# Backward pass of a transformer block: the gradient of w_qkv with its operands exchanged, and y's residual added by GpSimd

## The chip, the cores and the metric

The kernel runs on one core of one Trainium2 chip. The metric is the device time of one execution in microseconds (us); runs of one kernel are compared by the median. The engines are PE (TensorE, with PEld for its weight loads), DVE (VectorE), ACT (ScalarE), POOL (GpSimd) and SP (SyncE, which here only issues DMAs).

## What is computed

A block of attention and a gated feed-forward layer stand side by side on the normalised input, and the kernel returns the block's output and the gradients of six inputs for a given grad_out. S = 2048 rows, D = 448 columns, 16 heads of 28, F = 1792, all in bfloat16.

```python
def block(x, wqkv, wo, w_gate, w_up, w_down):
    xn = layernorm(x)
    q, k, v = split_heads(xn @ wqkv)          # 16 heads of 28
    p = softmax(q @ k.T * 28 ** -0.5)
    attention = merge_heads(p @ v) @ wo
    ffn = (silu(xn @ w_gate) * (xn @ w_up)) @ w_down
    return x + attention + ffn

out, vjp = jax.vjp(block, x, wqkv, wo, w_gate, w_up, w_down)
return (out, *vjp(grad_out))
```

The change touches two results: `out_2`, the gradient of wqkv (448 x 1344, xn transposed times the gradients of q, k and v), and `out_0`, the block's output y.

## The kernel before

A tile framework allocates the buffers and sets the semaphores; the order of the instructions on each engine is the one in which the code calls them. Heads are handled in four groups of four; each head is padded from 28 to 32 rows, so that a group fills 128 partitions. The rows of x are cut into 16 tiles of 128 (`NT`).

**Forward and feed-forward part** (up to about 673 us). Projections, the forward softmax and the feed-forward layer with its weight gradients. Its intermediate results go to DRAM: `hd_d` holds, per row tile, the transposed attention output and the transposed hidden activations; `qT_d`, `kT_d`, `vT_d`, `dOT_d` and `spq_d`, `spk_d`, `spo_d` hold what the backward attention reads.

**Backward loop** (lines 627 to 918). A unit is one pair of heads, one quarter (512) of the keys and one tile of 128 query rows; there are 512 units (`units`), and eight of them make a window `W`, with position `pos` 0 to 7 in it. Per unit PE computes scores and dP (`sd`, L851 and L862), ACT the exponential `E` (L869), DVE `ds` = dP times E (L880), and PE accumulates the gradients of k and v (`acc_mm`, L748, four matmuls on 32 columns of the array each). Six of eight `ds` tiles are transposed by DMA from SP (L882, `dsT<-ds`), the other two by PE (L775, copied out in L782); from `dsT` PE makes the gradient of q once per window (`dq_mm`, L795), and DVE adds it up (`dq_out`). There are eight `ds` buffers. When a pair is done, its gradients lie in `dsp[pr]`: `dkv_sp` with v and k by row tile (transposed by SP, L761) and `dq_sp` with q (L817).

**Jobs.** Other work for PE is spread over positions 1 to 4 of each window, one job a window by the list `jobs` (`None` is a window without one): `y` computes a row tile of the output, 18 matmuls of 448 columns and a nineteenth that adds x through the identity matrix; `dx` a row tile of two partial input gradients, 14 matmuls; `dwq` the gradient of wqkv for one group `g` and one chunk `c` of 128 of the 448 rows. Before, `dwq` has the chunk of xn as the weights and moves the gradients, 128 columns (k and v of one pair) or 64 (q of one pair) at a time. Its result (384 columns) is copied by ACT (`dwq_raw`), put in order by six POOL copies (`dwq_z`) and written by one DMA. A job's chunk of `hd_d` is loaded by SP two windows ahead (`job_load`, `ck` and `x_c`).

**SP's queue** carries, in this order of calls, the chunk loads at position 0, the loads of the next pair, group and weights (`load_pair`, `load_group`, `load_w`) at position 4, the `ds` transposes, and what is in the list `sp_later` (the transposes L761 and L817), which is emptied once a unit. In the built program each transfer of this queue also waits for the landing of an earlier one with which it shares a semaphore.

**The end** (lines 921 to 980). The fourth group's `dwq` is computed without a window, partly in the loop's last steps and partly after it (`last_dwq`), in two of the three PSUM buffers `sd`. Then come 16 rows of the input gradient: 2 + 12 matmuls of 448 columns on `pab` (partial sums) and `dq_c` (gradients of q, k, v from DRAM), a normalisation backward on ACT and DVE, and the addition of grad_out by POOL (`dx`, L979), written by SP. Their loads are issued by SP (`load_c` for chunks 0 to 2) and ACT.

Of the kernel before, what the change touches and what calls it, by code (L numbers as in the profile page):

```python
# [10 lines left out]
ALU = mybir.AluOpType  # L11
AX = mybir.AxisListType
FP32 = mybir.dt.float32
BF16 = mybir.dt.bfloat16
# [16 lines left out]
DCH = [(0, 128), (128, 128), (256, 128), (384, 64)]  # L31
# [6 lines left out]
def kernel(  # L38
# [19 lines left out]
    pe, act, dve, pool, sp = nc.tensor, nc.scalar, nc.vector, nc.gpsimd, nc.sync  # L58
# [22 lines left out]
    ident_bf = const.tile([P, P], BF16, name="ident_bf")  # L81
# [6 lines left out]
    xn_sp = const.tile([P, NT, DP], BF16, name="xn_sp")  # L88
# [39 lines left out]
    for b in (2, 3):  # L128
# [10 lines left out]
        out=r_ones[:], in_=ident_f[:].rearrange("p (a b) -> p a b", b=HP)[:, :, 28:30],  # L139
# [448 lines left out]
    for i, (g, qc, kt) in enumerate(steps):  # L588
# [24 lines left out]
        if i in (6, 8, 10, 12):  # L613
            j = i // 2 - 3
# [12 lines left out]
    cst = ExitStack()  # L627
    dspp = cst.enter_context(tc.tile_pool(name="dspp", bufs=3))
    outp = cst.enter_context(tc.tile_pool(name="outp", bufs=2))
    ps_sd = cst.enter_context(tc.tile_pool(name="ps_sd", bufs=3, space=PSUM))  # L630
    ps_x = cst.enter_context(tc.tile_pool(name="ps_x", bufs=1, space=PSUM))
    ast = ExitStack()
# [11 lines left out]
    N = len(units)  # L644
    NW = N // UW
    chunk, dsp, dqacc = {}, {}, {}


    jobs = [None] + [("y", t) for t in range(NT)] + [None] + [("dwq", 0, c) for c in range(4)]
    jobs += [("dx", 0, t) for t in range(NT)] + [("dwq", 1, c) for c in range(4)]  # L650
    jobs += [("dx", 1, t) for t in range(8)] + [None] + [("dwq", 2, c) for c in range(4)]
    jobs += [("dx", 1, t) for t in range(8, NT)]

    def job_load(i):
        if i >= len(jobs) or jobs[i] is None:
# [12 lines left out]

    def dwq_mms(g, c, ps):

        out = []
        lhs = lambda t: xn_sp[:, t, c * P:(c + 1) * P]

        def kvm(t):
            for hp in range(2):
                pe.matmul(ps[:, hp * P:(hp + 1) * P], lhsT=lhs(t), rhs=dsp[2 * g + hp][0][:, t, :],
                          start=(t == 0 and hp == 0), stop=(t == NT - 1), skip_group_check=True)

        def qm(t):
            for hp in range(2):  # L680
                pe.matmul(ps[:, 256 + hp * 64:256 + hp * 64 + 64], lhsT=lhs(t),
                          rhs=dsp[2 * g + hp][1][:, t // 8, t % 4, t % 8 // 4, :],
                          start=False, stop=(t == NT - 1), skip_group_check=True)
        for f in (kvm, qm):
            out.append([lambda t=t, f=f: f(t) for t in range(NT)])
        return out

    def dwq_out(g, c, ps):
        d0, dn = DCH[c]
        o = outp.tile([P, 384], BF16, name="dwq_raw")  # L690
        act.copy(out=o[:], in_=ps[:, :384])
        z = outp.tile([P, 3, 4, DH], BF16, name="dwq_z")
        kv = o[:, :256].rearrange("p (h v j r) -> p h v j r", h=2, v=2, r=HP)
        for tq in range(3):
            for hp in range(2):
                src = (o[:, 256 + 64 * hp:320 + 64 * hp].rearrange("p (j r) -> p j r", r=HP) if tq == 0
                       else kv[:, hp, 2 - tq])
                pool.tensor_copy(out=z[:, tq, 2 * hp:2 * hp + 2, :], in_=src[:, :, :DH])
        pool.dma_start(
            out=out_2[d0:d0 + dn, :].rearrange("p (t c) -> p t c", t=3)[:, :, g * 4 * DH:(g + 1) * 4 * DH],  # L700
            in_=z[:dn].rearrange("p t h d -> p t (h d)"))

    def job_mms(i, ps):
        j = jobs[i]
        if j[0] == "dwq":
            return sum(dwq_mms(j[1], j[2], ps), [])
        if j[0] == "y":
            t, x = chunk[i]
            out = []
            for n in range(NFC + G):  # L710
                rhs = (wo_pad[:, n, :D] if n < G else wtile["wd"][:, n - G, :])
                out.append(lambda n=n, rhs=rhs: pe.matmul(ps[:, :D], lhsT=t[:, n, :], rhs=rhs,  # L712
                                                          start=(n == 0), stop=False))
            out.append(lambda: pe.matmul(ps[:, :D], lhsT=ident_bf[:], rhs=x[:], start=False, stop=True))
            return out
        t = chunk[i]
        w = wtile[("wg", "wu")[j[1]]]
        return [lambda n=n: pe.matmul(ps[:, :D], lhsT=t[:, n, :], rhs=w[:, n, :],  # L718
                                      start=(n == 0), stop=(n == NFC - 1)) for n in range(NFC)]

    def job_out(i, ps):
        j = jobs[i]
        if j[0] == "dwq":
            dwq_out(j[1], j[2], ps)
            return
        o = outp.tile([P, D], BF16, name="row_o")
        act.copy(out=o[:], in_=ps[:, :D])
        if j[0] == "y":
            pool.dma_start(out=out0_d[:, j[1], :], in_=o[:])
        else:  # L730
            pool.dma_start(out=(pA_d, pB_d)[j[1]][:, j[2], :], in_=o[:])
        if j[0] != "dwq" and j[-1] == NT - 1 and j[:2] != ("dx", 1):
            wload.extend(load_w("wg" if j[0] == "y" else "wu", 7))

    E, DS, st = {}, {}, {}
    sp_later = []

    def acc_mm(k):
        pr, kc, w, qi = units[k]
# [89 lines left out]
    fillers, last_dwq = [], []  # L829
    for k in range(N + 2 * UW):  # L830
        W, pos = k // UW, k % UW
        if k < N:
            pr, kc, w, qi = units[k]
# [13 lines left out]
            q, kv = qd[pr]  # L847
            qt = 8 * w + qi
            s_ps = ps_sd.tile([P, 2, 512], FP32, name="sd")
            for j in range(2):  # L850
                pe.matmul(s_ps[:, j, :], lhsT=q[HP * j:HP * j + HP, qt * P:(qt + 1) * P],  # L851
                          rhs=kv[HP * j:HP * j + HP, kc * 512:(kc + 1) * 512],
                          start=True, stop=True, tile_position=(HP * j, 0))
        late_tr = pos == 0 and 1 <= W <= NW
        if 1 <= k <= N:
            pr, kc, w, qi = units[k - 1]
            q, kv = qd[pr]
            qt = 8 * w + qi
# [34 lines left out]
        if 1 <= pos < 5 and job:  # L893
            n = -(-len(fillers) // (5 - pos))
# [1 line left out]
                f()  # L896
            fillers = fillers[n:]
        if k == N + UW + 5:
            for c in range(4):
                if c % 2 == 0:  # L900
                    g_t = ps_sd.tile([P, 2, 512], FP32, name="sd")
                last_dwq.append((g_t[:, c % 2, :], dwq_mms(3, c, g_t[:, c % 2, :])))
            for _, m in last_dwq:
                for f in m[0][:12]:
                    f()
        if pos == 5 and 2 <= W <= NW + 1:
            dq_mm(W - 2, 0)
# [13 lines left out]
    with ExitStack() as fin:  # L921
# [17 lines left out]
            q.dma_start(out=dq_c[ck][:], in_=dqkv_d[ck])  # L939
        for ck in range(3):  # L940
            load_c(ck, sp)
        for part in range(2):
            for c, (ps, m) in enumerate(last_dwq):
                for f in m[part][12 * (1 - part):]:
                    f()
                if part == 1:
                    dwq_out(3, c, ps)
        wq = wtile["wq"]
        for t in range(NT):
            if t % 2 == 0:  # L950
# [61 lines left out]
```

## Time and profile before

| | |
|---|---|
| median of 3 runs | 1563.34 us (1561.85 to 1567.34) |
| profiled execution, its own time | 1562.89 us |
| span from its first to its last instruction | 1561.1 us |
| granted TensorE clock | 0.976 |
| PE, DVE, ACT, POOL busy | 93%, 70%, 76%, 25% of the span |
| DMA | 285.12 MB, mean 183 GB/s |
| SP's and ACT's transfers (q1) | 210.03 MB, 72.7% of 16 engines |
| first and last exponential of the backward loop | 673 and 1481 us |

A line of a group reads: source line, engine, operation, tile written <- tiles read with their sizes, number of instructions | busy us, mean ns of one | idle us of the engine just before them, and who ended most of it. "SPq" is SP's queue: an entry is the issue of a DMA, not its transfer; "to landing" is the time from issue until the data is there. A busy PE is not PE at its peak, since the ends of pipelined matmuls are modelled.

### The profile page before, as it was taken

To read this page: it belongs to the slowest core of one execution; us is meant where nothing else is said; L and a number is where in the kernel's file an instruction comes from. 1 tells how busy PE (TensorE), PEld (TensorE's weight loads), DVE (VectorE), ACT (ScalarE), POOL (GpSimd) and SP (SyncE) were. 2 spreads that over 40 slices of the span, in tenths; PEclk is the share of its full clock that TensorE was granted. 3 is DMA by queue.
4 is the path that set the end of the run, shared out by engine and by line. 5 is a ranking of instruction groups with operands and counts; after the bars stand their busy time and mean duration, and the time that the engine had idled before them with its cause. 6 is when DMAs were issued, how large, how long until landed. Compare 5 with 4: busy or idle time off the path is not lost.

```text
span 1561.1 us, 32024 instructions
## 1 busy us (share of the span) xinstructions
PE 1447.1 (93%) x12176; PEld 606.3 (39%) x12176; DVE 1098.9 (70%) x1421; ACT 1190.1 (76%) x1333; POOL 396.1 (25%) x664
## 2 busy tenths in 40 slices
PE   6999999899999999988998988989999899999986
PEld 3233333333333333333333444434335333544353
DVE  7664655455655666467877887979888789888925
ACT  6899998688787877766776777878778778888823
POOL 4342333344434444411010111110102111111033
PEclk9999999899999999989999999999999999999998
DMA  9985756875967699879999999999999999999993
GB/s 231 190 162 120 145 116 137 164 146 127 198 131 155 134 186 212 170 164 222 204 214 200 192 202 217 198 197 200 207 208 199 196 194 196 185 188 213 184 281 123
DMA packets 682106, 285.12 MB, mean 183 GB/s; under 512 B 637136, under 2 KB 650464, under 8 KB 681952
## 3 DMA queue, kind: packets, MB, share of 16 engines
q1 hardware_dynamic: 652016, 210.03, 72.7%
q0 software_dynamic: 25968, 64.53, 17.1%
q10 hardware_dynamic: 3968, 8.52, 1.6%
q8 instruction: 95, 1.56, 0.4%
q14 instruction: 59, 0.48, 0.1%
HBM read 67.34 MB, written 63.44 MB: 84 GB/s over the span
## 4 chain that ended last, share of the span: by engine, by line
PE 63%; DMA 14%; ACT 9%; DVE 6%; issue 5%; SPq 1%; POOL 1%; DVEq 0%; POOLq 0%; ACTq 0%
PE s_ps L600 8%; PE f_ps L357 8%; DMA dsT<-ds 8%; PE f_ps L383 7%; PE sd L851 6%; ACT E L869 5%; PE acc L748 4%; PE aux L718 4%; PE o_ps L582 4%; PE aux L775 4%; PE aux L795 4%; DVE ds L880 3%; PE aux L712 3%; ACT dsT L782 3%; PE sd L862 3%
## 5 line engine op out<-in xcount | busy, mean ns | idle before, releaser
L880 DVE TENSOR_TENSOR ds<-sd,E 128x1024 bf16<-128x1024 f32 x512 | 611.2, 1220 | 131.8 <-DMA dsT<-ds 47.8
L869 ACT ACTIVATE E<-sd 128x1024 bf16<-128x1024 f32 x512 | 516.7, 1024 | 171.7 <-PE sd L862 133.6
L604 ACT ACTIVATE eT<-s_ps 128x1024 bf16<-128x1024 f32 x512 | 497.9, 1024 | 103.8 <-PE s_ps L600 102.9
L862 PE MATMUL sd<-kT,qT 32*128 32x512 bf16 x1024 | 203.2, 390 | 23.6 <-ACT E L869 22.7
L851 PE MATMUL sd<-kT,qT 32*128 32x512 bf16 x1024 | 201.9, 391 | 20.1 <-DVE ds L880 17.9
L748 PE MATMUL acc<-ds,v_sp 128*32 128x512 bf16 x1024 | 205.7, 397 | 0.7 <-DVE ds L880 0.7
L748 PE MATMUL acc<-E,O_sp 128*32 128x512 bf16 x1024 | 205.5, 397 | 0.2 <-ACT dkv_o L754 0.2
L600 PE MATMUL s_ps<-qT,kT 32*128 32x512 bf16 x1024 | 200.1, 388 | 1.5 <-ACT eT L604 1.1
L422 POOL DMA_DIRECT2D hd_d<-fT x168 | 126.8, 767 | 17.2 <-DVE fT L407 9.9
L383 PE MATMUL f_ps<-xnT,wgu 128*128 128x512 bf16 x448 | 120.2, 387 | 3.4 <-DVE w_sb L409 3.4
L763 POOL DMA_DIRECT2D dqkv_d<-dkv_o x64 | 39.3, 619 | 293.1 <-ACT dkv_o L754 290.9
L600 PEld LDWEIGHTS <-kT 32*128 32x128 bf16 x1024 | 48.7, 91 | 159.8 <-issue 158.1
L718 PE MATMUL aux<-W,ck 128*128 128x448 bf16 x448 | 107.1, 356 | 3.3
L851 PEld LDWEIGHTS <-qT 32*128 32x128 bf16 x1024 | 51.0, 91 | 149.2 <-issue 141.2
L582 PE MATMUL o_ps<-eT,v_sp 128*32 128x512 bf16 x1024 | 103.2, 394 | 0.0
L357 PE MATMUL f_ps<-xn_sp,f_sp 128*128 128x448 bf16 x448 | 99.1, 354 | 0.0
L748 PEld LDWEIGHTS <-O_sp 128*32 128x32 bf16 x1024 | 50.4, 93 | 113.5 <-issue 103.7
L775 PE MATMUL aux<-ident_bf,ds 128*128 128x128 bf16 x1024 | 81.6, 224 | 11.6 <-DVE dq_acc L807 5.7
L862 PEld LDWEIGHTS <-qT 32*128 32x128 bf16 x1024 | 65.0, 91 | 61.7 <-issue 57.8
L357 PEld LDWEIGHTS <-f_sp 128*128 128x128 bf16 x672 | 58.3, 98 | 73.8 <-issue 23.7
L775 PEld LDWEIGHTS <-ds 128*128 128x128 bf16 x1024 | 63.7, 100 | 40.9 <-issue 40.2
L395 DVE SCALAR_TENSOR_TENSOR g<-t_sb,f_ps 128x512 f32<-128x512 f32 x56 | 38.5, 687 | 55.4 <-ACT t_sb L393 55.3
(133 smaller groups left out, 1759.8 us busy)
## 6 DMA issues: line engine op xcount, KB each, us to landing
hd_d<-fT POOLq DMA_DIRECT2D x168, 128.0 KB, 4.6
ck<-hd_d SPq DMA_DIRECT2D x32, 448.0 KB, 4.4
ck<-hd_d SPq DMA_DIRECT2D x16, 576.0 KB, 4.9
dsT<-ds SPq DMA_TRANSPOSE x384, 4.1
dqkv_d<-dkv_o POOLq DMA_DIRECT2D x64, 64.0 KB, 3.7
dq_c<-dqkv_d ACTq DMA_DIRECT2D x5, 768.0 KB, 6.8
W<-wT_d SPq DMA_DIRECT2D x14, 224.0 KB, 3.6
out_dram<-dw_o POOLq DMA_DIRECT2D x28, 96.0 KB, 4.0
```

The source lines that it names most:

```text
L357: pe.matmul(acc[:, :D], lhsT=src[:, 12 * (t // 4) + 4 * wi + t % 4, :], rhs=rhs[:, t, :D], start=(t == 0), stop=(t == NT - 1))
L383: pe.matmul(st[name][:], lhsT=w(c), rhs=src[:, tsl, c, :], start=(c == 0), stop=(c == 3))
L582: pe.matmul(o_ps[HP * hh:HP * (hh + 1), :], lhsT=v[:, kt, HP * hh:HP * (hh + 1)], rhs=e[hh // 2][:, hh % 2, :], start=(kt == 0), stop=(kt ...
L600: pe.matmul(s_ps[:, j, :], lhsT=kT[r:r + HP, kt * P:(kt + 1) * P], rhs=qT[r:r + HP, qc * 512:(qc + 1) * 512], start=True, stop=True, tile_ ...
L604: act.activation(out=e[:], in_=s_ps[:], func=ACT.Exp, scale=SCALE)
L718: return [lambda n=n: pe.matmul(ps[:, :D], lhsT=t[:, n, :], rhs=w[:, n, :], start=(n == 0), stop=(n == NFC - 1)) for n in range(NFC)]
L748: pe.matmul(acc[r:r + HP, :], lhsT=src[:, qt, 64 * hp + HP * j:64 * hp + HP * j + HP], rhs=m[:, j, :], start=(qt == 0), stop=(qt == NT - 1 ...
L775: pe.transpose(ps[:, i, :], ds[:, i // 4, (i % 4) * P:(i % 4 + 1) * P], ident_bf[:])
L851: pe.matmul(s_ps[:, j, :], lhsT=q[HP * j:HP * j + HP, qt * P:(qt + 1) * P], rhs=kv[HP * j:HP * j + HP, kc * 512:(kc + 1) * 512], start=Tru ...
L862: pe.matmul(d_ps[:, j, :], lhsT=q[r:r + HP, qt * P:(qt + 1) * P], rhs=kv[r:r + HP, kc * 512:(kc + 1) * 512], start=True, stop=True, tile_p ...
L869: act.activation(out=E[k][:], in_=s_ps[:], func=ACT.Exp, scale=SCALE)
L880: dve.tensor_tensor(out=DS[k - 1][:], in0=d_ps[:], in1=E[k - 1][:], op=ALU.mult)
```

## The change

The gradient of wqkv is computed transposed. For group `g` there are now three jobs instead of four: `c` = 0 and 1 are k and v of one pair (16 matmuls, the pair's 128 gradient columns are the weights and xn's 448 columns move), `c` = 2 is q of the whole group (64 matmuls, each with 32 columns of weights on a quarter of the array's columns). ACT copies the 448 columns of the result into one of two fixed buffers, `dwq_w[c % 2]`; SP transposes that by DMA into `dwq_o`; POOL copies the parts into `dwq_z`, and after `c` = 2 issues four DMAs that write the group. The transpose and what follows it are put off through `sp_later`, which is now declared ahead of the loop. The job list follows: windows without a job are 0, 17, 40 and 60 to 63 instead of 0, 17, 50 and 63, and the `dx` jobs start one window earlier. At the end the fourth group's three jobs are worked off one after the other, each with its transposes issued at once.

In `y`, the nineteenth matmul is gone. ACT copies the sum in FP32 (`y_sb`), POOL adds x and writes `row_o`, and the DMA follows as before.

```diff
+    gwp = cst.enter_context(tc.tile_pool(name="gwp", bufs=1))
...
-    jobs = [None] + [("y", t) for t in range(NT)] + [None] + [("dwq", 0, c) for c in range(4)]
-    jobs += [("dx", 0, t) for t in range(NT)] + [("dwq", 1, c) for c in range(4)]
-    jobs += [("dx", 1, t) for t in range(8)] + [None] + [("dwq", 2, c) for c in range(4)]
-    jobs += [("dx", 1, t) for t in range(8, NT)]
+    sp_later = []
+    dwq_w = [gwp.tile([P, DP], BF16, name=f"dwq_w{i}") for i in range(2)]
+    for w in dwq_w:
+        pool.memset(w[:, D:], 0.0)
+    jobs = [None] + [("y", t) for t in range(NT)] + [None] + [("dwq", 0, c) for c in range(3)]
+    jobs += [("dx", 0, t) for t in range(NT)] + [("dwq", 1, c) for c in range(3)] + [None]
+    jobs += [("dx", 1, t) for t in range(9)] + [("dwq", 2, c) for c in range(3)]
+    jobs += [("dx", 1, t) for t in range(9, NT)]
...
         def kvm(t):
-            for hp in range(2):
-                pe.matmul(ps[:, hp * P:(hp + 1) * P], lhsT=lhs(t), rhs=dsp[2 * g + hp][0][:, t, :],
-                          start=(t == 0 and hp == 0), stop=(t == NT - 1), skip_group_check=True)
+            pe.matmul(ps[:, :D], lhsT=dsp[2 * g + c][0][:, t, :], rhs=xn_sp[:, t, :D],
+                      start=(t == 0), stop=(t == NT - 1))
 
         def qm(t):
-            for hp in range(2):
-                pe.matmul(ps[:, 256 + hp * 64:256 + hp * 64 + 64], lhsT=lhs(t),
-                          rhs=dsp[2 * g + hp][1][:, t // 8, t % 4, t % 8 // 4, :],
-                          start=False, stop=(t == NT - 1), skip_group_check=True)
+            for h in range(4):
+                pe.matmul(ps[HP * h:HP * (h + 1), :D],
+                          lhsT=dsp[2 * g + h // 2][1][:, t // 8, t % 4, t % 8 // 4, HP * (h % 2):HP * (h % 2 + 1)],
+                          rhs=xn_sp[:, t, :D], start=(t == 0), stop=(t == NT - 1),
+                          tile_position=(0, HP * h), skip_group_check=True)
+        return [lambda t=t: (kvm if c < 2 else qm)(t) for t in range(NT)]
...
     def dwq_out(g, c, ps):
...
+        w = dwq_w[c % 2]
+        act.copy(out=w[:, :D], in_=ps[:, :D])
+        if c == 0:
+            dwq_z[g] = gwp.tile([P, 4, 3, 4, DH], BF16, name="dwq_z")
+        z = dwq_z[g]
+        o = outp.tile([P, 4, P], BF16, name="dwq_o")
+        def later():
+            sp.dma_start_transpose(out=o[:], in_=w[:])
+            parts = [(0, 0, 4, 0)] if c == 2 else [(2, 2 * c, 2, 0), (1, 2 * c, 2, 64)]
+            for tq, h0, n, c0 in parts:
+                pool.tensor_copy(out=z[:, :, tq, h0:h0 + n, :],
+                                 in_=o[:, :, c0:c0 + HP * n].rearrange("p c (h r) -> p c h r", r=HP)[:, :, :, :DH])
+            if c < 2:
+                return
+            for i, (d0, dn) in enumerate(DCH):
+                pool.dma_start(
+                    out=out_2[d0:d0 + dn, :].rearrange("p (t c) -> p t c", t=3)[:, :, g * 4 * DH:(g + 1) * 4 * DH],
+                    in_=z[:dn, i].rearrange("p t h d -> p t (h d)"))
+        sp_later.append(later)
...
-            out.append(lambda: pe.matmul(ps[:, :D], lhsT=ident_bf[:], rhs=x[:], start=False, stop=True))
...
-        act.copy(out=o[:], in_=ps[:, :D])
+        if j[0] == "y":
+            y = outp.tile([P, D], FP32, name="y_sb")
+            act.copy(out=y[:], in_=ps[:, :D])
+            pool.tensor_tensor(out=o[:], in0=y[:], in1=chunk[i][1][:], op=ALU.add)
+        else:
+            act.copy(out=o[:], in_=ps[:, :D])
...
-            for _, m in last_dwq:
-                for f in m[0][:12]:
+            for _, m in last_dwq[:2]:
+                for f in m[:12]:
                     f()
...
-        for part in range(2):
-            for c, (ps, m) in enumerate(last_dwq):
-                for f in m[part][12 * (1 - part):]:
-                    f()
-                if part == 1:
-                    dwq_out(3, c, ps)
+        for c, (ps, m) in enumerate(last_dwq):
+            for f in m[12 if c < 2 else 0:]:
+                f()
+            dwq_out(3, c, ps)
+            while sp_later:
+                sp_later.pop(0)()
```

More of the change, by code (lines that the diff above doesn't have):

```diff
@@ L669, in dwq_mms @@
     def dwq_mms(g, c, ps):
-        out = []
-        lhs = lambda t: xn_sp[:, t, c * P:(c + 1) * P]
         def kvm(t):
-            for hp in range(2):
-                pe.matmul(ps[:, hp * P:(hp + 1) * P], lhsT=lhs(t), rhs=dsp[2 * g + hp][0][:, t, :],
-                          start=(t == 0 and hp == 0), stop=(t == NT - 1), skip_group_check=True)
+            pe.matmul(ps[:, :D], lhsT=dsp[2 * g + c][0][:, t, :], rhs=xn_sp[:, t, :D],
+                      start=(t == 0), stop=(t == NT - 1))
@@ L679, in qm @@
         def qm(t):
-            for hp in range(2):
-                pe.matmul(ps[:, 256 + hp * 64:256 + hp * 64 + 64], lhsT=lhs(t),
-                          rhs=dsp[2 * g + hp][1][:, t // 8, t % 4, t % 8 // 4, :],
-                          start=False, stop=(t == NT - 1), skip_group_check=True)
-        for f in (kvm, qm):
-            out.append([lambda t=t, f=f: f(t) for t in range(NT)])
-        return out
-    def dwq_out(g, c, ps):
[L689 to L701, printed above, removed]
@@ new lines, in qm @@
+            for h in range(4):
[4 more added lines that the diff above has]
+        return [lambda t=t: (kvm if c < 2 else qm)(t) for t in range(NT)]
+    dwq_z = {}
+    def dwq_out(g, c, ps):
+        w = dwq_w[c % 2]
[17 more added lines that the diff above has]
+        sp_later.append(later)
@@ L705, in job_mms @@
         if j[0] == "dwq":
-            return sum(dwq_mms(j[1], j[2], ps), [])
+            return dwq_mms(j[1], j[2], ps)
         if j[0] == "y":
-            t, x = chunk[i]
+            t = chunk[i][0]
             out = []
@@ L712, in job_mms @@
                 out.append(lambda n=n, rhs=rhs: pe.matmul(ps[:, :D], lhsT=t[:, n, :], rhs=rhs,
-                                                          start=(n == 0), stop=False))
-            out.append(lambda: pe.matmul(ps[:, :D], lhsT=ident_bf[:], rhs=x[:], start=False, stop=True))
+                                                          start=(n == 0), stop=(n == NFC + G - 1)))
             return out
@@ L735 @@
     E, DS, st = {}, {}, {}
-    sp_later = []
     def acc_mm(k):
@@ L898 @@
         if k == N + UW + 5:
-            for c in range(4):
+            for c in range(3):
                 if c % 2 == 0:
```

## The prediction

> **What bounds the kernel now.** I read the page first, then a table of stretches, then SyncE's queue, then the tail. The page says PE is busy nearly everywhere, but DMA engines too:
>
> ```profile
> PE 1447.1 (93%) x12176; PEld 606.3 (39%) x12176; DVE 1098.9 (70%) x1421; ACT 1190.1 (76%) x1333; POOL 396.1 (25%) x664
> DMA  9985756875967699879999999999999999999993
> L880 DVE TENSOR_TENSOR ds<-sd,E 128x1024 bf16<-128x1024 f32 x512 | 611.2, 1220 | 131.8 <-DMA dsT<-ds 47.8
> ```
>
> The change lies in the backward loop (from 673 us) and in what follows it. I cut the loop into its 64 windows of eight units, each from its second exponential (ACT L869) to the next one's in the timeline. Free windows repeat to a few ns: 10.94 us without a job (W50), 11.78 and 12.05 in turn with a dx job, 11.88 and 12.15 with a dwq job, 12.48 and 12.54 with a y job (W15, W16). The stretches show which are not free (columns: us; busy us of PE, PEld, DVE, ACT, POOL; clock, DMA share, GB/s):
>
> ```profile
> 686.70:900.50 213.80, 194.24 (x1828) 81.93 (x1829) 168.38 (x160) 155.55 (x169) 22.55 (x38) 0.99 1.06 207
> 912.00:967.90 55.90, 48.34 (x644) 26.42 (x641) 42.88 (x41) 38.71 (x44) 9.49 (x32) 0.94 1.06 208
> 1169.30:1217.30 48.00, 46.06 (x644) 26.26 (x640) 41.61 (x40) 38.67 (x43) 11.95 (x36) 1.00 1.07 196
> 1217.30:1318.60 101.30, 91.31 (x884) 37.99 (x881) 85.34 (x82) 78.25 (x86) 11.88 (x20) 1.00 1.06 198
> 1318.60:1329.50 10.90, 9.05 (x100) 3.52 (x96) 10.39 (x12) 9.23 (x11) 1.20 (x2) 1.00 1.09 170
> 1329.50:1377.60 48.10, 46.18 (x644) 26.36 (x641) 42.53 (x42) 38.77 (x44) 9.51 (x32) 1.00 1.06 187
> 1377.60:1472.90 95.30, 92.04 (x884) 38.80 (x881) 84.94 (x81) 78.13 (x86) 11.88 (x20) 1.00 1.05 196
> ```
>
> The same four dwq windows (rows 2, 3, 6) take 55.9, 48.0 and 48.1 us; the same eight dx1 windows (rows 4, 7) 101.3 and 95.3. PE's work is equal, so the longer ones wait for something else. In the first dwq stretch it is SyncE's queue, which issues without a pause:
>
> ```profile
> 941.36 4.17 SPq L882 DMA_TRANSPOSE dsT<-ds  x3
> 945.58 1.14 SPq L666 DMA_DIRECT2D ck<-hd_d  x1
> 946.82 5.58 SPq L882 DMA_TRANSPOSE dsT<-ds  x3
> 952.49 1.24 SPq L761 DMA_TRANSPOSE dkv_sp<-dkv_o  x1
> 953.78 0.57 SPq L564 DMA_DIRECT2D O_sp<-spo_d  x1
> 954.40 0.42 SPq L540 DMA_DIRECT2D W<-wT_d  x1
> 954.92 4.36 SPq L882 DMA_TRANSPOSE dsT<-ds  x3
> ```
>
> A ds buffer (eight of them) is free when its transpose has landed; once SyncE is about eight units late, L880 waits (the 47.8 us above). So the loop has two regimes: PE's pace where SyncE keeps up, SyncE's where loads of pairs, groups and weights pile up (W1 to W14, W18 to W28, W33 to W36, W41 to W45).
>
> **The change, part by part.** *dwq on PE.* 448-column matmuls follow each other at 0.189 us (a tail row of 14 takes 2.65 us), 128-column ones at 0.057 (96 of L676 in 5.46 us of the chain), 64-column ones in the loop at 0.030 (16 in 0.64 us, the last of them 0.19 long). A dwq job before is 32 x 0.057 + 32 x 0.030 = 2.8 us, a kv job after is 16 x 0.189 = 3.02. The q job has 64 matmuls on 32 columns of the array, four at a time: the nearest row is L795, 16 such of 512 columns in 0.98 us, so 16 x 0.245 x 448/512 = 3.4 us. The Trainium skill, "TensorEngine Tiling (Array Packing)", section Restrictions, says that column tiling turns Fast Weight Load off. If each load then showed (64 at the 93 ns of L748's), a q job would be 6.0 us and the sum up to 8 us higher; but L795's 0.98 us contains its sixteen loads, so I keep 3.4. Fitted between a dx window (14 x 0.189) and a y window (19), the new windows come to about 12.2 us, 0.2 above the old.
>
> There are nine such windows in the loop instead of twelve, and empty ones are 0, 17, 40 and 60 to 63 instead of 0, 17, 50, 63. In W46 to W63, where SyncE keeps up, before is 12 x 11.915 + 4 x 12.015 + 2 x 10.94 = 212.9 us and after 11 x 11.915 + 3 x 12.2 + 4 x 10.94 = 211.4: **-1.5**. In SyncE's stretches a PE saving is worth nothing.
>
> *y on PE.* One matmul of 0.189 us less in 16 windows: 3.0 at most. y windows average 13.36 (213.8/16) against 12.5 free, and even free windows hang on ACT in their third unit, so only four or five can use it: **-0.2** (-1.2 to 0). The add (POOL, 1.04 us as L979) and its DMA are read by nobody in the loop; x_c is released later but has three buffers.
>
> *Transposes on SyncE.* Three per group, each 1.19 us (L369, the same shape) to 1.24 (L761) plus 0.09 us to the next issue: 1.3. DMA_TRANSPOSE comes behind the ds transposes, and the ds transposes behind it. They wait for ACT's copy, which ends before SyncE gets there. POOL's copies wait for them, with row_o and dkv DMAs queued behind, which have two buffers and a window's time: 0. POOL's own work falls (six copies of 0.23 per chunk to five per group), four output DMAs of 0.68 are the same number.
> First group: three transposes in a full queue, 3.9, and with one window less ahead of dx0 one chunk load (L666, 0.57 to 1.14) enters it: **+4.6** (0 to +6). Second group: 3.9 us in W37 to W39, just ahead of the pile in W41 to W45, which then starts fuller; but those windows had SyncE gaps of some 0.5 us each and dx0's last chunk leaves the pile of W33 to W36 a window sooner: **+2.0** (0 to +4.6). Third: the queue is short there (no stall in W48 to W54), yet chunk loads resume at W51 instead of W53: **+0.3** (0 to +3).
>
> *The tail.* Before dq_mm of the last window PE does 24 x 0.189 = 4.5 us instead of 5.5: everything behind shifts by -0.9. Then q waits for the last dq_sp transpose, lands, and the rows begin:
>
> ```profile
> 1499.20 0.96 PE L681 MATMUL sd<-dq_sp,xn_sp 128*128 128x64 bf16 x15 [5.04 <-DMA dq_sp<-dq_o]
> 1500.78 3.57 PE L681 MATMUL sd<-dq_sp,xn_sp 128*128 128x64 bf16 x64 [0.62 <-ACT dwq_raw L691]
> 1504.99 1.09 PE L681 MATMUL sd<-dq_sp,xn_sp 128*128 128x64 bf16 x32 [0.64 <-ACT dwq_raw L691]
> ...
> 1511.22 0.54 PE L956 MATMUL sd<-pab,ident_bf 128*128 128x448 bf16 x2
> ```
>
> After, q needs 1.7 us once the transpose has landed, so rows could start near 1503 (dq_c of chunk 0 lands at 1495.5 + 8.4 = 1503.9 less 0.9) instead of 1505.9. But ACT's third copy writes dwq_w0 and must wait until its first transpose has read it, and that transpose is issued behind pab and dq_c loads which land in the order of issue, the last 12.2 us after 1499.24: 1511.4. Less 0.9, plus about 0.8 for the transpose (half of a ds one): 1511.3. ACT holds everything behind that copy: the first rows' g_sb, and the PSUM buffer of the third row, whose matmuls then start at 1511.9 where they started at 1511.22. **+0.7** (-3.0, if the transpose comes at once, to +3.0, if POOL's late copies and four DMAs hold the first dx adds long enough to be felt).
>
> Sum: -1.5 - 0.2 + 4.6 + 2.0 + 0.3 + 0.7 = **+5.9 us**. The profiled execution took 1562.89 us (span 1561.1), the median is 1563.34, so one sum serves both: 1569.
>
> **The rivals.** *SyncE has room* (faster): the new transposes fill gaps, as the 256 us in which L882 waited for its ds would allow, and land in the tail ahead of the loads. Then -1.5 - 1.2 - 3.0: 1557.6. It decides at dwq_w0's last transpose landing before about 1504 and at first-group windows not above 12.2 us. Against it: the queue excerpt above is 97% issue. 0.14. *The tail gains, the loop loses*: +5.2 - 3.0 gives 1565.5; it needs landing out of order. 0.2. *Every group pays in full*: 4.6 + 4.6 + 3, with -1.5 + 0.7 and 1.5 of further stalls, 1576. For it: the pile at W41 is fed directly. 0.15. *POOL's add holds DVE*: in the tail L976, two SBUF operands, took up to 1.48 us instead of 0.68 while L979 ran. The add starts some 0.3 us after ACT's copy, beside L880; if that were held for all of 16 x 1.04 us, less what PE-bound windows hide, some 8 us more: 1577. L880 reads PSUM and never took over 1.23 us, also beside POOL's copies: 0.05. The Trainium skill, "GPSIMD Engine Reference", section Key points, puts the conflict at DVE instructions with two SBUF inputs or in a 2-port mode, which fits both rows. The forecast keeps 0.46.
>
> **The numbers.** The likeliest case gives 1569. The range 1560 to 1577 takes in the tail's gain and full payment, and leaves out most of the first rival and of the last. About 0.3% (4.7 us) is what a measurement of this kernel can tell from no change. Slower: three quarters of the forecast and the two dear rivals, 0.55; within: the rest of the forecast and the tail's gain, 0.33; faster: 0.12.
>
> **What would show it.** Right: dwq windows 18 to 20 of 14 to 16 us with SyncE issuing throughout and more L880 waits on dsT; W60 to W62 near 10.94; q matmuls in groups of four at about 0.2 us; ACT's third tail copy ending near 1511 on the old scale, and the third row no earlier than before. Wrong: W18 to W20 near 12.2 us, or tail rows running through from 1503, or L880 above 1.23 us in y windows.

## The result, and the profile after

The changed kernel takes 1574.29 us (median of 11 runs, 1567.78 to 1585.15), the kernel before 1561.85 us beside it (11 runs): ratio 1.0092, 95% interval [1.0068, 1.0116], slower by some 12 us (the ratio is not the quotient of the two medians, which is 1.0080). The profiled execution took 1576.7 us, its span is 1574.9 us, the granted clock 0.978 (before 0.976). The lines of the page that answer to those of before:

```profile
PE 1435.8 (91%) x11520; PEld 571.3 (36%) x11520; DVE 1099.5 (70%) x1421; ACT 1188.9 (75%) x1329; POOL 402.4 (26%) x606
DMA  8975857967777699699999999999999999999993
L893 DVE TENSOR_TENSOR ds<-sd,E 128x1024 bf16<-128x1024 f32 x512 | 609.9, 1220 | 150.1 <-DMA dsT<-ds 90.3
```

PE is busy for 11 us less, and the span is 14 us longer. What grew is the last number of the third line: the time for which DVE's `ds` stood because a transpose had not landed, 47.8 us before and 90.3 now. That sum differs much from profile to profile: in the first two experiments below it is 69.9 us with the same transposes and 67.7 without those of the loop. Only its part in W50 to W54, shown further down, is clear. (`ds`, L880 before, is L893 now; the exponential L882, the `ds` transposes L895, the new transposes L700.)

The windows, cut as in the prediction, from one profiled execution each. "No transposes" and "old slots" are two experiments below.

| us | before | after | no transposes | old slots |
|---|---|---|---|---|
| first exponential | 673.4 | 667.7 | 664.8 | 662.3 |
| W1 to W16 | 213.7 | 215.6 | 212.5 | 214.0 |
| W17 to W25 | 115.1 | 118.4 | 117.6 | 118.4 |
| W26 to W36 | 142.0 | 141.3 | 139.8 | 142.1 |
| W37 to W45 | 113.4 | 119.2 | 116.4 | 117.7 |
| W46 to W49 | 47.6 | 47.9 | 47.7 | 47.7 |
| W50 to W54 | 59.0 | 66.3 | 60.2 | 59.9 |
| W55 to W59 | 59.4 | 59.4 | 59.4 | 60.8 |
| W60 to W62 | 35.9 | 34.6 | 33.7 | 35.9 |
| last exponential to the end | 80.4 | 83.3 | 83.5 | 86.0 |

One warning goes with the table. W1 to W16 carry no transposes of the change, and over the eleven profiled kernels whose loads SyncE issues they lie between 205 and 219 us; the first exponential lies between 662 and 677. A difference of 2 or 3 us in such a row is nothing. W46 to W59 repeat within a fraction of a microsecond where nothing disturbs them, so their rows can be read.

The stretch that grew most is W50 to W54. Its first three windows (the third group's dwq) and the two dx windows behind them (columns as in the prediction):

```profile
1323.50:1362.90 39.40, 34.15 (x388) 13.70 (x385) 31.27 (x30) 29.57 (x33) 3.71 (x8) 1.00 1.05 184
1362.90:1389.80 26.90, 22.47 (x224) 8.94 (x221) 21.28 (x22) 19.59 (x23) 5.76 (x9) 1.00 1.02 195
1389.80:1449.20 59.40, 57.42 (x550) 24.22 (x551) 53.27 (x51) 48.45 (x54) 7.69 (x13) 1.00 1.04 194
1449.20:1483.80 34.60, 27.50 (x292) 10.83 (x289) 31.19 (x31) 27.41 (x31) 2.42 (x4) 1.00 1.10 192
```

The fourth row is W60 to W62, now without jobs, where PE works 27.50 us; the third is five undisturbed dx windows. In the first two rows PE is idle for 5.3 and 4.4 us with the clock at 1.00. Two of the waits of this stretch (total us, times, longest) stand first, two of the same stretch before below them. DVE's wait for a landed `ds` transpose, 12.4 us here, does not occur there before:

```profile
POOL dwq_z L703 <- DMA dwq_o<-dwq_w: 37.4, 3, 14.3
DVE ds L893 <- DMA dsT<-ds: 12.4, 7, 2.5
```

```profile
POOL dqkv_d L763 <- ACT dkv_o L754: 20.9, 3, 7.8
DVE ds L880 <- PE sd L862: 3.9, 9, 0.5
```

And SyncE's queue in W51 and W52 has no gap of more than 0.12 us. From W51 into W52:

```profile
1336.81 1.26 SPq L895 DMA_TRANSPOSE dsT<-ds  x1
1338.18 2.16 SPq L700 DMA_TRANSPOSE dwq_o<-dwq_w  x1
1340.43 2.63 SPq L895 DMA_TRANSPOSE dsT<-ds  x2
1343.12 0.57 SPq L671 DMA_DIRECT2D ck<-hd_d  x1
1343.78 4.86 SPq L895 DMA_TRANSPOSE dsT<-ds  x3
1348.69 1.24 SPq L553 DMA_DIRECT2D kT<-vT_d  x2
1350.03 1.26 SPq L895 DMA_TRANSPOSE dsT<-ds  x1
1351.39 1.20 SPq L700 DMA_TRANSPOSE dwq_o<-dwq_w  x1
```

A transpose of a result (L700), a chunk load (L671) and the next pair's loads (L553) stand together in it. In the kernel before, windows 48 to 52 load no chunk for a coming window.

The tail. ACT, then POOL and DVE:

```profile
1519.78 0.53 ACT L693 CAST dwq_w<-sd 128x448 bf16<-128x448 f32 x1 [15.13 <-DMA dwq_o<-dwq_w]
1532.51 0.72 ACT L987 ACTIVATE t<-sd,bb,rstd 128x448 f32<-128x448 f32 x1 [4.16 <-DVE cc L984]
```

```profile
1525.01 0.62 POOL L703 COPY dwq_z<-dwq_o 128x448 bf16<-128x448 bf16 x1 [3.96 <-DMA dwq_o<-dwq_w]
1525.93 2.82 POOL L708 DMA_DIRECT2D out_dram<-dwq_z  x4 [0.30 <-POOL dwq_z L703]
1528.38 2.40 POOL L992 TENSOR_TENSOR dx<-t,dy_t 128x448 bf16<-128x448 f32 x2
```

```profile
1524.53 0.69 DVE L989 SCALAR_TENSOR_TENSOR t<-xn_sp,cc,t 128x448 f32<-128x448 bf16 x1 [0.67 <-ACT t L987]
1527.86 3.42 DVE L989 SCALAR_TENSOR_TENSOR t<-xn_sp,cc,t 128x448 f32<-128x448 bf16 x1 [0.67 <-ACT t L987]
```

ACT's third copy waits 15.13 us for the first transpose to have read its buffer, as foreseen. POOL then has the last copy and the group's four DMAs ahead of the first dx sum. Beside the last of these issues and the first two sums, DVE's L989 takes 3.42 us instead of 0.69 and ends 0.5 us after the second sum; behind it ACT waits 4.16 us. Measured from the last exponential, the first dx sum begins at 36.8 us (before 32.8) and the last at 76.0 (before 73.1).

### The profile page after: what moved, and what is told of

It is laid out like the page before. It is cut to its first block, busy times and chain, and to the rows that moved or that the text cites. A ratio compares the mean times of both kernels' runs of the same rounds, so it can differ in the third digit from the quotient of the medians.

```text
span 1574.9 us, 30652 instructions
## 1 busy us (share of the span) xinstructions
PE 1435.8 (91%) x11520; PEld 571.3 (36%) x11520; DVE 1099.5 (70%) x1421; ACT 1188.9 (75%) x1329; POOL 402.4 (26%) x606
## 4 chain that ended last, share of the span: by engine, by line
PE 55%; DMA 19%; DVE 10%; ACT 8%; issue 6%; POOL 1%; SPq 1%; DVEq 0%; POOLq 0%; ACTq 0%
DMA dsT<-ds 13%; PE s_ps L600 8%; PE f_ps L357 8%; PE f_ps L383 7%; DVE ds L893 6%; PE sd L864 5%; PE o_ps L582 4%; PE aux L727 4%; ACT E L882 4%; PE acc L761 3%; PE aux L788 3%; PE aux L808 3%; PE f_ps L180 3%; PE aux L722 2%; PE sd L875 2%
## 5 line engine op out<-in xcount | busy, mean ns | idle before, releaser
L893 DVE TENSOR_TENSOR ds<-sd,E 128x1024 bf16<-128x1024 f32 x512 | 609.9, 1220 | 150.1 <-DMA dsT<-ds 90.3
L882 ACT ACTIVATE E<-sd 128x1024 bf16<-128x1024 f32 x512 | 516.5, 1023 | 191.9 <-PE sd L875 156.0
L875 PEld LDWEIGHTS <-qT 32*128 32x128 bf16 x1024 | 65.0, 91 | 63.9 <-issue 60.8
L788 PEld LDWEIGHTS <-ds 128*128 128x128 bf16 x1024 | 63.3, 99 | 47.6 <-issue 47.1
```

The lines of the kernel that those rows point to most:

```text
L788: pe.transpose(ps[:, i, :], ds[:, i // 4, (i % 4) * P:(i % 4 + 1) * P], ident_bf[:])
L882: act.activation(out=E[k][:], in_=s_ps[:], func=ACT.Exp, scale=SCALE)
L893: dve.tensor_tensor(out=DS[k - 1][:], in0=d_ps[:], in1=E[k - 1][:], op=ALU.mult)
```

## The experiments

Each ran in five rounds beside the kernel before; a ratio is to that. Three theories were open: that the added work is dear in itself (POOL's add, or the transposes), that the order of the jobs is, or that the nine transposes have no room in SyncE's queue.

### y's residual back on TensorE

```diff
-                  start=(n == 0), stop=(n == NFC + G - 1)))
+                  start=(n == 0), stop=False))
+  out.append(lambda: pe.matmul(ps[:, :D], lhsT=ident_bf[:], rhs=x[:], start=False, stop=True))
...
-            pool.tensor_tensor(out=o[:], in0=y[:], in1=chunk[i][1][:], op=ALU.add)
+        act.copy(out=o[:], in_=ps[:, :D])
```

> The changed kernel with y's half of the change taken back: PE adds x through the identity matrix again, POOL adds nothing. Queue theory (the loss is the DMA transposes on SyncE's queue): the ratio to the kernel before stays at 1.009, within 0.003, and L880's counterpart waits on dsT as long as in the changed kernel (90 us against 48). Job-order theory (the loss is that chunk loads now meet the loads of pairs and groups): also 1.009. POOL theory (the add on POOL or the FP32 copy costs the loss): 1.004 or less, with shorter y windows.

Measured: 1577.86 us, ratio 1.0130 [1.0085, 1.0175]. Undoing this part gains nothing, so POOL's add is not the loss. The ratio lies a little higher than expected, and the wait on `dsT` is 69.9 us and not 90; in W50 to W54 it is 8.3 us.

### The nine transposes of the loop left out

```diff
-        o = outp.tile([P, 4, P], BF16, name="dwq_o")
+        o = outp.tile([P, 4, P], BF16, name="dwq_o") if g == 3 else w[:].rearrange("p (c k) -> p c k", c=4)
...
-            sp.dma_start_transpose(out=o[:], in_=w[:])
+            if g == 3:
+                sp.dma_start_transpose(out=o[:], in_=w[:])
```

> The changed kernel without the nine DMA transposes of the loop: POOL copies straight out of ACT's buffer, so out_2 of the first three groups is left in the wrong layout; the fourth group, in the tail, is as in the changed kernel. Queue theory: 12 us come back or nearly so, ratio 0.999 to 1.003, the windows of the second and third dwq group at 12.0 to 12.3 us, and the wait on dsT back at about 50 us. Job-order theory: at most 3 us come back, 1.007 to 1.009. POOL theory: 1.009.

Measured: 1558.99 us, ratio 0.9996 [0.9968, 1.0025]. The whole loss goes with the nine transposes (and POOL's wait for them): 15 us, 1.7 us each. The table's W50 to W54 falls from 66.3 to 60.2, and of DVE's 12.4 us of waiting there this is left:

```profile
DVE ds L894 <- DMA dsT<-ds: 0.5, 1, 0.5
```

Over the whole kernel that wait does not go back to about 50 us, as expected, but to 67.7, with a time as before: the sum over all windows is no measure of the loss. The tail keeps its 83.5 us, since the last group's three transposes are still there.

### The old places of the jobs

```diff
-... [("dwq", 0, c) for c in range(3)]
+... [("dwq", 0, c) for c in range(3)] + [None]
-    jobs += [("dx", 1, t) for t in range(9)] + [("dwq", 2, c) for c in range(3)]
-    jobs += [("dx", 1, t) for t in range(9, NT)]
+    jobs += [("dx", 1, t) for t in range(8)] + [None] + [("dwq", 2, c) for c in range(3)] + [None]
+    jobs += [("dx", 1, t) for t in range(8, NT)]
```

> The changed kernel with the job list of before: the fourth place of each dwq group is a window without a job, so that every y and dx job and every chunk load stands in its old window. Nothing is left out. Queue theory: 1.006 to 1.010, since all twelve transposes are still there. Job-order theory: 1.001 to 1.004; the piles at windows 40 to 45 and 50 to 54 go back to their lengths of before (about 101 and 48 us). POOL theory: 1.009.

Measured: 1568.29 us, ratio 1.0064 [1.0038, 1.0089]. It still carries all transposes, and W50 to W54 takes 59.9 us. That stretch is 66.3 us in the changed kernel and 66.0 in the first experiment, which have the new order; 60.2 without transposes and 59.9 here. So the 6 us there need both: the transposes, and the new order, which puts chunk loads beside them. DVE's wait on `dsT` in this stretch says the same: 12.4 us in the changed kernel and 8.3 in the first experiment, at most 0.5 before, without transposes and here. POOL's wait for the transposes is as long here as in the changed kernel (37.4 us) and costs nothing in this stretch:

```profile
POOL dwq_z L703 <- DMA dwq_o<-dwq_w: 41.4, 3, 21.5
```

Not separated: the old list has no chunk load in W50 to W52, and it also has two windows without a job, W50 and W54. Over the whole kernel the difference of 0.0028 between the two ratios is within their intervals, and W37 to W45 did not go back to its old length (117.7 us, before 113.4).

### Nine idle transposes in the kernel before

```diff
+    extra_w = gwp.tile([P, DP], BF16, name="extra_w")
+    pool.memset(extra_w[:], 0.0)
...
+        if g < 3 and c < 3:
+            x_o = outp.tile([P, 4, P], BF16, name="extra_o")
+            sp_later.append(lambda: sp.dma_start_transpose(out=x_o[:], in_=extra_w[:]))
```

> The kernel before, with nine DMA transposes more on SyncE's queue, of a fixed 128x512 tile into a tile that nobody reads, three in each dwq group of the loop at the place where the changed kernel has them; all else is as before. Queue theory: 1.005 to 1.009 (8 to 14 us). Job-order theory and POOL theory: 1.000 to 1.002.

Measured: 1566.32 us, ratio 1.0044 [1.0015, 1.0072]. Nine transposes that nobody waits for cost about 7 us, with everything else as before. This is the cost of their place in the queue alone, about half of the loss and a little less than expected. W50 to W54 takes 59.9 us with them and 59.0 without.

### One transpose per group

```diff
+        if g < 3:
+            act.copy(out=dwq_w3[:, c, :D], in_=ps[:, :D])
+            if c < 2:
+                return
...
+                sp.dma_start_transpose(out=o3[:], in_=dwq_w3[:].rearrange("p c d -> p (c d)"))
```

> The changed kernel, but the three results of a group in the loop stand in one tile and are transposed by one DMA behind the third (3 issues instead of 9, the same bytes); the last group is left as it is. Two theories of where the cost of the nine transposes (15 us between the changed kernel and the one without them) comes from. By issue: SyncE has no free 1.2 us in those windows, so six issues fewer give back about two thirds: about 1564 us, 1.003 of before, and dwq windows of the second and third group of at most 13 us. By byte: the transposing DMA engines are what is full, and the same packets must go through: about 1574 us, 1.009 of before, the loss gathered behind the third result of each group.

### A quarter of the bytes

```diff
-            sp.dma_start_transpose(out=o[:], in_=w[:])
+            if g == 3:
+                sp.dma_start_transpose(out=o[:], in_=w[:])
+            else:
+                sp.dma_start_transpose(out=o[:, 0, :], in_=w[:, :P])
```

with two fixed tiles `dwq_q` for the result; the rest of the transposed rows is left out.

> The changed kernel, but each of the nine transposes in the loop moves only the first 128 of 512 columns (the same nine issues, a quarter of the bytes); the rest of the gradient's rows of those groups is left out, POOL's copies and stores are as before. By issue: if an issue costs SyncE the same whatever it moves, nothing is gained, about 1574 us, 1.009 of before. By byte: three quarters of the packets are gone, about 1563 us, 1.002 of before. If a transpose's issue is itself as long as it has columns, this one also comes out near 1563 and the kernel with one transpose per group at 1574: the row of the issue in the trace then tells which.

Measured: one per group 1567.00 us, 1.0060 [1.0031, 1.0089]; a quarter of the bytes 1574.97 us, 1.0100 [1.0066, 1.0134]. The rows of the issues (duration min/median/max in ns), of the changed kernel, of the first and of the second:

```profile
L700 SPq DMA_TRANSPOSE dwq_o<-dwq_w x12: 1188/1228/4783, 925.6 to 1520.5; - x12
```

```profile
L712 SPq DMA_TRANSPOSE dwq_o<-dwq_w x3: 1438/1700/2539, 952.2 to 1353.0; - x3
```

```profile
L706 SPq DMA_TRANSPOSE dwq_q<-dwq_w x9: 1171/1183/2005, 933.5 to 1373.0; - x9
```

With a quarter of the bytes an issue takes 1183 ns instead of 1228 and nothing is gained: by byte is refuted. (That profiled execution took 1590.6 us, 16 more than the median.) With a third of the issues and three times the bytes in each, 1700 ns at the median, SyncE spends some 6 us less (the loop's nine add up to 12.0, the three to 5.7), and the medians differ by 8 us. So it is the issue that counts, which is almost as long for little as for much; but the two intervals overlap by a little, and 1.0060 is more than the 1.003 expected. That three issues still leave 1.0060 is more than their 5.7 us; the interval reaches down to 4.8 us, so this is not settled.

### The transposes put off to quiet windows

```diff
-        sp_later.append(later)
+        (dwq_defer if g < 3 else dwq_tail).append(later)
...
+        if pos == 4 and (46 <= W <= 48 or 56 <= W <= 61):
+            sp_later.append(dwq_defer.pop(0))
...
+            if t in (4, 6, 8):
+                dwq_tail.pop(0)()
```

with six buffers `dwq_w` instead of two.

> A version meant to beat both: the changed kernel with the nine transposes of the loop moved to windows without the dear loads (the first group's to windows 46 to 48, the other two to 56 to 61, one each), and the last group's three sent behind the fifth, seventh and ninth row of the tail from three buffers, so that ScalarE's third copy does not wait. If the place of the transposes is the cost, the windows 17 to 54 stand as in the kernel without transposes (117.6, 139.8, 116.4, 47.7 and 60.2 us), 55 to 62 stay at 11.9 us, and with a tail 3 us shorter than the changed kernel's it takes 1553 to 1560 us, 0.995 to 0.999 of before. If a transpose costs its 1.2 us and more wherever it stands, windows 46 to 48 and 56 to 61 become longer by 1 to 2 us each and it takes 1566 to 1572 us, 1.004 to 1.008.

Measured: 1573.00 us, ratio 1.0075 [1.0038, 1.0111]. It fails as an improvement, and its one profile suggests why. W46 to W48 themselves stay at 12.04, 11.78 and 12.05 us. The debt comes due a little later, in W50, when the next pair's loads meet the delayed queue; windows W50, and W55 to W59, and W60 to W62:

```profile
1313.90:1332.00 18.10, 13.12 (x116) 4.76 (x117) 11.71 (x12) 10.12 (x13) 3.49 (x6) 0.91 0.95 177
1380.90:1441.30 60.40, 57.45 (x554) 24.28 (x551) 53.00 (x50) 48.49 (x54) 12.29 (x22) 1.00 1.10 183
1441.30:1477.50 36.20, 29.25 (x289) 10.86 (x289) 30.48 (x30) 27.62 (x31) 7.10 (x13) 0.91 1.06 194
```

W50 takes 18.1 us, against 12.2 without transposes, W55 to W59 1.0 us more than before, W60 to W62 2.5 us more than without transposes. (The clock stands at 0.91 in the first and third row; a tenth of the 13.1 us for which PE works in W50 would be 1.3 us by my estimate, so it does not make up the 6.) SyncE's queue leading into W50:

```profile
1304.78 1.24 SPq L701 DMA_TRANSPOSE dwq_o<-dwq_w  x1
1306.11 1.27 SPq L896 DMA_TRANSPOSE dsT<-ds  x1
1307.42 1.28 SPq L831 DMA_TRANSPOSE dq_sp<-dq_o  x1
1308.80 6.03 SPq L896 DMA_TRANSPOSE dsT<-ds  x4
1314.88 3.19 SPq L553 DMA_DIRECT2D kT<-kT_d  x2
1318.16 4.27 SPq L896 DMA_TRANSPOSE dsT<-ds  x2
```

Two loads stand 3.19 us, where two of the same line take 1.24 in the excerpt of the changed kernel above, and two `ds` transposes 4.27, where two take 2.63. A window that runs at PE's pace isn't one in which SyncE's queue is empty: within W46 to W49 its issues stand for 44.4 of 47.6 us before, for 44.6 of 47.9 in the changed kernel and for 44.8 of 48.0 with the deferred transposes.

### y alone

The kernel before with only the second part of the change (the diff of the first experiment, the other way round).

> The kernel before with only y's residual moved from TensorE to POOL. The prediction's term: -0.2 us (-1.2 to 0), so 1.000 of before (0.999 to 1.001), windows 1 to 16 as long as before. If POOL's add held VectorE or POOL's own queue, 1.003 or more.

Measured: 1559.91 us, ratio 0.9993 [0.9963, 1.0024]. No effect that can be measured, as the term of -0.2 us said.

### The jobs' loads issued by POOL, after and before

```diff
-            sp.dma_start(out=t[:], in_=hd_d[j[1], :, :G + NFC, :])
+            pool.dma_start(out=t[:], in_=hd_d[j[1], :, :G + NFC, :])
-            sp.dma_start(out=x[:], in_=x_d[:, j[1], :])
+            pool.dma_start(out=x[:], in_=x_d[:, j[1], :])
```

and the same for the dx chunks, once in the changed kernel and once in the kernel before.

> The changed kernel, but the loads of the jobs (48 hidden or dx chunks and 16 of x) are issued by POOL instead of SyncE. Theory: SyncE is the bound of the whole loop (its issue times fill 0.91 to 0.95 of nearly every stretch of windows, before and after), so any place freed in its queue is time: 64 issues of about 0.57 us are 36 us, of which the windows can give back what they stand above the 11.9 us of undisturbed ones (16 windows at 13.5, 20 at 12.9 to 13.2): 20 to 30 us, so 1545 to 1555 us, 0.988 to 0.996 of before. Rival, that the transposes cost by landing order, bytes or the group's four stores, whatever else SyncE does: 1570 us or more, 1.006 or more.

> The same move of the jobs' loads to POOL in the kernel before. Theory: 1540 to 1550 us, 0.986 to 0.993 of before; and with room made in SyncE's queue the nine transposes of the changed kernel cost less, so that the kernel above stands at most 8 us behind this one, against 12 to 15 us with the loads on SyncE. If the cost of the transposes has nothing to do with the room in SyncE's queue, the distance stays 12 to 15 us.

Measured: changed kernel 1613.57 us, 1.0358 [1.0326, 1.0390]; kernel before 1598.95 us, 1.0241 [1.0201, 1.0281]. I had expected a gain and got 40 us of loss in both, each against its own form with the loads on SyncE. The reason can be read from the queue. In the changed kernel so altered, W26:

```profile
1029.27 1.70 SPq L553 DMA_DIRECT2D kT<-kT_d  x2
1031.07 8.80 SPq L895 DMA_TRANSPOSE dsT<-ds  x2
1039.93 1.90 SPq L830 DMA_TRANSPOSE dq_sp<-dq_o  x1
1041.92 10.02 SPq L895 DMA_TRANSPOSE dsT<-ds  x4
```

Two `ds` transposes take 8.80 us of SyncE, and four 10.02; one alone takes 1.30 at the median of this run, 1.23 at the least and 7.44 at the most. From the records of the kernel before: a `ds` transpose that overlaps a chunk load lands on average 4.44 us after its issue, one that doesn't 3.96; with the loads on POOL 5.81 and 3.99. The mean issue of all 384 grows from 1.52 to 1.73 us. Late chunks are not the reason: in the kernel before with POOL's loads the engines wait 1.6 us in all for a chunk, and DVE waits 95.4 us on `dsT` instead of 47.8. So no room was made: SyncE's issues still fill 0.93 to 0.94 of each stretch from W1 to W45, since an issue also contains waiting; what it waits for, the records don't tell. That refutes the reading of the first of the two expectations, in which the share of issue time was taken as work that could be moved away. It doesn't test whether room in the queue would make the transposes cheap. The distance between the two kernels, 14.6 us, is the old one.

### The tail put right

```diff
+        o = outp.tile([P, 4, P], BF16, name="dwq_o") if g < 3 else tail_o[c]
+        def turn():
+            sp.dma_start_transpose(out=o[:], in_=w[:])
...
+        if g == 3:
+            turn()
+        (sp_later if g < 3 else dwq_tail).append(later)
...
+            if t in (5, 7, 9):
+                dwq_tail.pop(0)()
```

with three buffers `dwq_w` instead of two and a tile `tail_o` for each of the last three results.

First with the loads on POOL, then as the new form in the last group alone (the loop's groups and job order as before, y on POOL).

> The first kernel of this call with the tail put right: three buffers for the last group, so that ScalarE's third copy does not wait, its three transposes where they are, and POOL's copies and stores of it behind rows 6, 8 and 10 instead of ahead of the first dx sum. Theory: the time from the last exponential to the end falls from 83.3 us to 77 to 80, the loop is as in the first kernel, so 3 to 6 us less than that. If instead the early rows are paced by the loads of the tail, the end comes no earlier than 83 us after the last exponential.

> The kernel before with the new form in the last group alone (its three results in the tail, with three buffers, POOL's copies and stores of them behind rows 6, 8 and 10), and y's residual on POOL; the three groups in the loop and the order of the jobs stay as before. Theory: the loop carries no transpose more, so it stands as in the kernel before; the tail falls from 80.4 us (before) and 83.3 us (the changed kernel) to 76.3 to 79. That is 1.5 to 4 us less than before: 1555 to 1558 us, 0.997 to 0.999. If the tail's gain in the kernel with POOL's loads came from its emptier SyncE queue and not from the order of POOL's work, the tail stays at 80 us or more and the ratio at 1.000.

Measured: the first 1601.78 us, 1.0255 [1.0210, 1.0301], with 76.3 us from the last exponential to the end instead of 81.1 without the tail's change. Its median fell by 11.8 us, more than those 4.8; the rest lies in the loop, which the edit touches only by the third `dwq_w` buffer, and I can't explain it. The second 1558.03 us, 1.0014 [0.9995, 1.0034], with a tail of 79.7 us, where 76.3 to 79 was expected. ACT doesn't wait for a buffer any more; its first row comes at once after PE:

```profile
1504.04 0.54 ACT L1015 ACTIVATE g_sb<-sd 128x448 bf16<-128x448 f32 x1 [6.51 <-PE sd L1011]
```

The third buffer and the later place of POOL's work together thus take back what the changed kernel's tail had lost (83.3 against 79.7 us); which of the two does it isn't separated. Against the kernel before only 0.7 us is left, and the 76.3 us belong to the loads on POOL: the kernel before with these loads has a tail of 75.6. In the second of the two runs POOL issues its four DMAs from 1534.86 to 1537.71, and DVE's instruction of the kind that took 3.42 us runs beside them in its usual time:

```profile
1534.99 0.69 DVE L1029 SCALAR_TENSOR_TENSOR t<-xn_sp,cc,t 128x448 f32<-128x448 bf16 x1 [0.85 <-ACT t L1027]
```

So the issues alone do not hold DVE up. The next one, at 1537.21, takes 0.68 us although POOL's two sums begin 0.1 us behind it; why the one in the changed kernel stood for both sums is not shown. No version that I ran beats the kernel before by an amount that can be measured.

## Why the prediction was right, and where it was not

The direction and the range (1560 to 1577) held; the point, 1569, is 5 us low. The median rose by 12.4 us, the sum said 5.9: the range took the result in because it had been made wide enough for the rivals, not because the terms were right. The nearest case was not the forecast but the rival "every group pays in full", 1576, to which I gave 0.15.

- **PE in free windows, -1.5.** Right: W46 to W62 without the transposes takes 201.0 us against 201.9 before, and W61 and W62 of the changed kernel took 10.77 and 10.94 us (W60, where I had also said 10.94, took 12.91). The saving is there, some 0.9 us, within what single profiles can tell.
- **The q matmuls on 32 columns.** Right: in the tail 34 take 1.88 us and 30 take 1.69, about 0.22 us for four, where the prediction took 0.21; loads of 0.093 us each on top don't show. The Trainium skill, "TensorEngine Tiling (Array Packing)", section Restrictions, has column tiling turn Fast Weight Load off; the rows show no price of it here.
- **y, -0.2.** Nothing measurable alone (0.9993), nor was its rival: `ds` stayed at 1220 ns.
- **First and second group, +4.6 and +2.0.** W17 to W25 and W37 to W45 grew by 3.3 and 5.8 us. That is near the sum, but not by the mechanism I gave alone: without transposes these stretches still stand 2.5 and 3.0 us above the one profile of before, which is no more than what profiled executions differ by. W18 to W20 took 12.28, 16.88 and 13.63 us, where I had said 14 to 16 each, and without the transposes 12.22, 17.26 and 13.47. That sign proved nothing. An estimate from more profiles: without transposes in these stretches (before, no transposes, put off, y alone, tail only) they take 117.0 and 114.8 us on average, with nine single ones (changed, first, old slots, idle, a quarter of the bytes) 118.8 and 117.4. So the first group pays some 2 us where I had said 4.6, and the second some 2.6.
- **Third group, +0.3 (0 to +3).** This is the term that failed: W50 to W54 grew by 7.3 us, 6.1 of them by the transposes (against 60.2 in the same order without them). I wrote that "the queue is short there" because nothing stalls in those windows before. A queue without stalls need not have room: SyncE's issues stand for 54.3 of those 59.0 us. Of the two things that I saw, three transposes and chunk loads from W51 on, each was small alone (60.2 us with the order, 59.9 with the transposes), and together they cost 6 us. I had added them up instead of asking what happens when both meet the next pair's loads.
- **The tail, +0.7 (-3 to +3).** It cost 2.9 us, the upper end (83.3 to 86.0 us in the six profiles of this form of the tail with the loads on SyncE, 79.7 to 80.4 in three of the old one). The trace shows the cause that I had named for that end. The wait of ACT's third copy came as predicted (15.13 us, ended by the landing of the first transpose), but on the scale of before it ran at 1508.9, not at 1511.3, so the third row was 1.8 us earlier than before. What stands there are POOL's last copy and four DMAs ahead of the first dx sums, and DVE's 3.42 us beside two sums in a row. The Trainium skill, "GPSIMD Engine Reference", section Key points, names the conflict for DVE instructions with two SBUF inputs; the row agrees (0.69 us alone), and is dearer than the 1.48 us that I had found before.

## What to carry to other kernels

Before a transfer is added to a queue, add up the issue times of that queue over the windows around it: the kernel before showed no stall in W46 to W54, and its queue was nine tenths full. But that share alone does not give the price: it is 0.91 to 0.93 in every stretch of the loop before up to W59, stalled or not, and three more transposes in W50 to W54 cost 0.9 us in the old order and 6 in the new. Two additions to one queue have to be tried together. The cost followed the number of issues here and not the bytes, and to move the transposes to calmer windows did not save it. And a share of issue time is not work that can be carried off to another engine, since part of it is waiting: measure the waiting transfers with and without the neighbour that is to go.

## What I had not expected of the hardware

- The issue of a transpose by SyncE is nearly as long for little as for much: 1.18 us for 128 columns, 1.23 for 512, 1.29 for the 1024 of a `ds` tile (medians), and 1.44 at the least for 1536 (1.70 the middle one of three).
- The same chunk loads disturb `ds` transposes more when POOL issues them than when SyncE does (landing at 5.81 against 4.44 us where they overlap), and they land later themselves, 5.8 and 6.7 us against 4.4 and 4.9 (medians of the DMA issues, both of the kernel before).
- A DVE instruction of 0.69 us took 3.42 to 3.44 us beside two sums that POOL made one after the other from SBUF, in seven profiles; beside POOL's issue of DMAs alone it took 0.69.
